# Regrouping the attention part of a fused attention and MLP kernel: two bursts a head in place of four

## The chip, the cores and the metric

The kernel runs on one core of a Trainium2 chip. The metric is the device time of one execution in microseconds (us). The engines are TensorE (PE in the profile, with its weight loads apart as PEld), VectorE (DVE), ScalarE (ACT), GpSimd (POOL) and SyncE (SP). Each runs its instructions in the order in which they were issued to it; a transfer is issued by one of their queues, nearly always SP's.

## The reference

```python
def _attn_ref(q, k, v, proj):              # 2 batches, 8 heads, 768 positions, 64 wide
    q_bits = (einsum('bhsd,dk->bhsk', q, proj) > 0)      # 6 bits; k_bits in the same way
    mask = q_bucket[:, :, :, None] == k_bucket[:, :, None, :]
    scores = where(mask, 1/sqrt(D) * q @ k.T, -1e9)
    attn = exp(scores - scores.max(-1))
    return attn / (attn.sum(-1) + 1e-9) @ v
# x: (1536, 512), the heads side by side
x = g1(x @ w_in) @ w_out        # 512 -> 2048 -> 512, g1(h) = h * tanh(softplus(h))
y = g2(x @ w2_in) @ w2_out      # the same sizes, g2 a rational function of h
```

## The kernel before

The attention part takes the first third of the time: 16 heads, one behind the other. The two MLP layers follow as 96 steps of 24 matmuls (3 blocks of 512 tokens, 16 slices of the hidden width, 2 layers).

**Numbers.** A large matmul splits each operand into a high and a low fp32r half and adds three products. The products P·V, the denominators and the hash codes are plain fp32, for which TensorE runs two instructions each. They use part of its columns: P·V (`both`, L285) and the codes two tiles of 64 columns side by side, the denominators (`dsum`, L400) four tiles of 32.

**Slots.** A head has six slots (`order`, L539, and the loop under it). Slot g of the whole run holds a list of operations, in the order of the rows of `order`; a row's first number says at which slot, counted from the head's own first, it stands, and its second how many there are (0: one for two heads). `slot_ops(g)` issues them, so each engine's queue has them in this order. In each slot TensorE computes a chunk of 128 keys of one head: `st` (L373) makes the scores `sp`, and ScalarE takes their exp `e`. For a later head, `smax` (L340) makes the products `mp`, whose row maxima VectorE reduces (`m`). Scores, maxima's products and a small sum of V (`vsum`, L268, tile `vsp`, read by VectorE as `vsc`) take turns in three PSUM buffers of two banks (`ps`, L181). P·V has one bank (`pv`), and the codes and denominators share one (`dn`, L182).

**Where things stand.** Per head, P·V stands in slots 3, 5 and 7, two chunks each; the denominators in slots 5 (two pairs of chunks) and 7 (one); the codes of a later head in slot 2 modulo 6 (`codes`, L298), with `code_k` on VectorE (L320) in the same slot and `code_q` on ScalarE (L329) two slots later. `hi` and `lo` split a head's q and k. `move_k`, `move_x` and `move_h` (L239 to L251) copy the halves between partitions by transfers. `fin_a` and `fin_b` (L354, L362) send the maxima back as a row of `qB`, through SP and GpSimd. `evac` and `devac` (L414, L427) take P·V and the denominators out of PSUM, and `gather`, `recip`, `store` and `spread` turn the latter into a factor for each position. For each pair of heads `norm`, `xhi` and `xlo` (L478 to L499) write the halves of the MLP's input; `norm` and `xhi` stand in slot 11 modulo 12, `xlo` in 5, `vsum` in 3. `weights` (L517) converts 14 parts of the MLP's weights, one a head: load, three VectorE instructions, split on GpSimd.

**Beginning and end.** `start` (L603) is a list by hand that prepares heads 0 to 2, with small products (`warm`) between. `tail` (L626) issues the last slots, from 99 on, within steps 1, 2 and 4 of the MLP; there VectorE also converts the rest of the first layer's weights (`direct_bits`, L777), which come through a ring of loads.

Of the kernel before, what the change touches and what calls it, by code (L numbers as in the profile page):

```python
# [9 lines left out]
F32 = mybir.dt.float32  # L10
# [16 lines left out]
BIG = 2.0 ** 40  # L27
NBITS = 6
EARLY, SHARED, FIRST = 7, 3, (78, 66, 72, 60, 60, 60, 60)
W_AT, W_LEAD = 7, 4  # L30
POOL_LO = (("lo", 1), ("lo", 2))
ENG = dict(
    lo="dd", hi="aa", xhi="a", xlo="dd", whi="pppp", wlo="pppp",
# [11 lines left out]
def attention_moe_moe(ctx: ExitStack, tc: tile.TileContext, kq, v, proj2, cst, eye, w1, w2, ab, out):  # L45
# [124 lines left out]
    def attention(actx, tctx):  # L170
# [26 lines left out]
        def memsets():  # L197
            nc.vector.memset(ones, 1.0)
            nc.vector.memset(wones, 1.0)
            nc.gpsimd.memset(cs_t, 0.0)  # L200
            nc.gpsimd.memset(cs_t[:, 1:2], -1.0)
            nc.gpsimd.memset(cs_t[:, 2:3], 1.0)
            for i in range(4):
                nc.gpsimd.memset(f32(KK[i])[32:64, 0], 0.0)
            for i in range(2):
                nc.gpsimd.memset(f32(SM[i]), 0.0)
            nc.gpsimd.memset(bias[:, 1:2], 1.000001)
# [25 lines left out]
                fn = fn or lo_of("lo", h)  # L233
                fn(qX[h % 4], raws[h], qB[h % 4])

        def khi(h, i):
            nc.scalar.activation(out=KK[h % 4][64:128, i], in_=raws[h][0:64], func=ACT.Copy)

        def move_k(h):  # L239
            if 0 <= h < B * H:  # L240
# [53 lines left out]

        ct = {}


        def codes(h):  # L298
            if not 0 <= h < B * H:
                return  # L300
            ct[h] = [pvp.tile([128, 512], F32, tag="dn", name="cp")] * 2
            if h == 0:
                ct[h][1] = pvp.tile([128, 512], F32, tag="pv", name="wm")
            for t in ct[h][0:1 + (h == 0)]:
                both(t, p_raw, raws[h], start=True, stop=True)


        warm_up = []

        def warm(n):  # L310
            if 0 in ct:
                t = ct[0][1]
            else:
                if not warm_up:
                    warm_up.append(ps.tile([128, 2, 512], F32, tag="s", name="wm"))
                t = warm_up[0][:, 0]
            for _ in range(n):
                nc.tensor.matmul(out=t[0:32, HALF:512], lhsT=ones, rhs=wones, start=True, stop=True)

        def code_k(h):  # L320
            if not 0 <= h < B * H:
                return
            for a in range(2):
                nc.vector.tensor_scalar(
                    out=qhalf(KK[h % 4][0:32, 0], a), in0=ct[h][0][64 * a:64 * a + 32, 0:HALF],
                    scalar1=cs_t[:, 1:2], scalar2=cs_t[:, 2:3], op0=ALU.is_gt, op1=ALU.mult,
                )

        def code_q(h):  # L329
            if not 0 <= h < B * H:  # L330
                return
            for a in range(2):
                nc.scalar.activation(
                    out=qhalf(qB[h % 4], a)[0:32], in_=ct[h][1][64 * a + 32:64 * a + 64, 0:HALF],
                    func=ACT.Sign, bias=cs_t[:, 0:1],
                )

        mt = {}

# [58 lines left out]


        def dsum(h, c):  # L400
            if not 0 <= h < B * H or c % 2 == 0:
                return
            if c == 1:
                pvt[h, "d"] = pvp.tile([128, 512], F32, tag="dn", name="dn")
            for n in range(4):
                nc.tensor.matmul(  # L406
                    out=pvt[h, "d"][32 * n:32 * n + 32, 0:HALF], lhsT=ones, rhs=qhalf(pt[h, c - 1 + n // 2], n % 2),
                    start=(c == 1), stop=(c == NC - 1),
                )

        Rt = {}
# [15 lines left out]
        def devac(h):  # L427
            if not 0 <= h < B * H:
                return
            dv = cs_p.tile([128, HALF], F32, tag="dv", name="dv")  # L430
            nc.scalar.activation(out=dv, in_=pvt.pop((h, "d"))[:, 0:HALF], func=ACT.Copy)
            Rt[h] = dv

        def gather(h):
            if not 0 <= h < B * H:
                return
            dv = Rt.pop(h)
            cs = cs_p.tile([24, 2, 32], F32, tag="cs", name="cs")
            for n in range(2):
                nc.sync.dma_start(  # L440
                    out=cs[:, n], in_=dv[64 * n:64 * n + 64:32].rearrange("t (a i) -> t a i", i=32)
                )
            Rt[h] = cs

        def recip(h):
            if not 0 <= h < B * H:
                return
            cs = Rt.pop(h)
            rc = cs_p.tile([24, 32], F32, tag="rc", name="rc")

            z = cs_p.tile([24, 32], F32, tag="z", name="z")
            nc.vector.tensor_tensor(out=rc, in0=cs[:, 0], in1=cs[:, 1], op=ALU.add)
            nc.vector.tensor_scalar(
                out=z, in0=rc, scalar1=0.0, scalar2=float(np.float32(1e-9)) / (S * TINY) - 1.0, op0=ALU.is_equal, op1=ALU.mult
            )
            nc.vector.tensor_scalar(out=rc, in0=rc, scalar1=1e-9, scalar2=None, op0=ALU.add)
            nc.vector.reciprocal(out=rc, in_=rc)
            nc.vector.scalar_tensor_tensor(out=rc, in0=z, scalar=1.0, in1=rc, op0=ALU.add, op1=ALU.mult)
            Rt[h, "r"] = rc
# [64 lines left out]
        def first(f, n):  # L524
# [16 lines left out]
            ("smax", smax, -11, 6),  # L541
            ("fin_a", fin_a, -5, 1),
            ("fin_b", fin_b, -5, 1),
            ("hi", hi, -18, 1),
            ("move_k", move_k, -17, 1),
            ("lo", lo, -15, 1),
            ("codes", codes, -16, 1),
            ("pv", pv, (3, 3, 5, 5, 7, 7), 6),
            ("dsum", dsum, (5, 5, 5, 5, 7, 7), 6),
            ("vsum", vsum, 3, 0),  # L550
            ("code_k", code_k, -16, 1),
            ("code_q", code_q, -14, 1),
            ("evac", evac, 7, 1),
            ("devac", devac, 7, 1),
            ("gather", gather, 8, 1),
            ("recip", recip, 10, 1),
            ("store", store, 11, 1),
            ("spread", spread, 12, 1),
            ("norm", norm, 23, 0),
            ("xhi", xhi, 23, 0),  # L560
            ("xlo", xlo, 29, 0),
            ("vred", vred, -6, 0),
            ("move_x", move_x, -13, 1),
            ("move_h", move_h, -11, 1),
# [2 lines left out]
            ("weights", weights, 0, -1),  # L567
            ("first", first, FIRST, -2),
        )
        last = 6 * nh + 3  # L570
        slots = {}
        done = set()
        for name, fn, at, per in order:
# [3 lines left out]
                todo = [(at[c] + 6 * h, (h, c)) for h in range(nh) for c in range(per)]  # L577
            elif name == "smax":
                todo = [((at, c - 2, 4 + c)[h] if h < 3 else at + 6 * h + c, (h, c)) for h in range(nh) for c in range(per)]
            elif name.startswith("fin_"):  # L580
                todo = [((at, 3, 9)[h] if h < 3 else at + 6 * h, (h,)) for h in range(nh)]
            elif per > 0:
                todo = [(at + 6 * h + c, (h, c) if per > 1 else (h,)) for h in range(nh) for c in range(per)]
            elif per == 0:
                todo = [(at + 12 * j, (j,)) for j in range(nh // 2)]
            else:
                todo = [(g, (g,)) for g in range(6 * nh)]
# [7 lines left out]

        def get(i):
            t, d = ((p_raw, proj2), (cs_t[0:31], cst[0:31]), (ab_t, ab))[i]
            nc.sync.dma_start(out=t, in_=d)

        def coef():  # L600
            nc.scalar.activation(out=babs, in_=ab_t[:, 4:6], func=ACT.Abs)

        start = (  # L603
            ("load", 0), ("get", 0), ("get", 1), ("load", 1), ("load", 2), ("warm", 5), ("hi", 0), ("codes", 0),
            ("khi", 0, 0), ("lo", 0), ("code_q", 0), ("code_k", 0), ("warm", 1), ("hi", 1), ("lo", 1), ("khi", 0, 1),
            ("get", 2), ("move_x", 0), ("smax", 0, 0), ("warm", 2), ("move_h", 0), ("hi", 2), ("lo", 2), ("smax", 0, 1),
            ("move_k", 1), ("warm", 2), ("smax", 0, 2), ("load", 3), ("warm", 2), ("smax", 0, 3), ("codes", 1),
            ("smax", 0, 4), ("warm", 2), ("code_q", 1), ("smax", 0, 5), ("fin_a", 0), ("fin_b", 0), ("code_k", 1),
            ("warm", 6), ("move_k", 2), ("load_v", 0), ("move_x", 1), ("smax", 1, 0), ("smax", 1, 1), ("move_h", 1),
            ("coef",),  # L610
        )

        def run():
            memsets()
            fns = {o[0]: o[1] for o in order}
            fns.update(get=get, coef=coef, khi=khi)
            for name, *k in start:
                if name == "warm":
                    warm(*k)
                    continue  # L620
                done.add(("move_k" if name == "khi" else name, tuple(k[:1]) if name == "khi" else tuple(k)))
                fns[name](*k, **({"fn": lo_pool} if (name, *k) in POOL_LO else {}))
            for g in range(last):
                slot_ops(g)

        def tail(i):  # L626
            for g in {1: range(last, last + 3), 2: range(last + 3, last + 5), 4: range(last + 5, last + 30)}.get(i, ()):
                slot_ops(g)

        return run, tail  # L630
# [1 line left out]
    def moe(mctx, tctx, tail):  # L632
# [114 lines left out]
        def run():  # L747
# [70 lines left out]
            for i in range(-5, len(seq) + 5):  # L818
# [20 lines left out]
                        fn(*k)  # L839
                if i >= 0:  # L840
                    tail(i)
                if i == 4:
                    tctx.close()
                for group in ((ring_store, slot_lo, direct_lo), (slot_both, slot_f32, direct_load, ring_load)):
                    for fn, k in now:
# [75 lines left out]
```

## Time and profile before

| | |
|---|---|
| median of 3 runs | 793.95 us (792.95 to 795.28) |
| the profiled execution | 791.69 us, span 789.8 |
| PE, PEld busy | 774.2 us (98%), 572.4 us (72%) |
| DVE, ACT, POOL busy | 593.7 us, 422.5 us, 71.6 us |
| chain that ended last | PE 88%, DVE 6%, DMA 2% |
| attention, MLP | to 259.65 us, from there to the end |

Times in the profile's views are us from the beginning of the span. A busy share alone doesn't say whether an engine runs well: TensorE may be busy with products that change its tiling, and a wait may lie on the one engine that sets the end. An instruction in a line is named by engine, source line, and "out<-in" of its tiles; "x8" says that eight in a row were merged.

### The profile page before, as it was taken

How to read it: one execution, taken by the hardware profiler on the slowest of the kernel's cores; microseconds unless marked ns; L12 is line 12 of the kernel's file. 1: busy time of each engine (PE TensorE's matmuls, PEld its weight loads, DVE VectorE, ACT ScalarE, POOL GpSimd, SP SyncE). 2: the span in 40 equal slices, each digit the busy share in tenths (PEclk: the TensorE clock that was granted, in tenths of full speed). 3: DMA queues.
4: the chain of work that ended last, by engine and by line, in shares of the span. 5: the costliest groups of instructions: out<-in, count | busy, mean ns of one | idle time of the engine just before them, and what ended most of it. 6: DMA issues, size and time to landing. Idle time of an engine off the chain costs nothing.

```text
span 789.8 us, 10934 instructions
## 1 busy us (share of the span) xinstructions
PE 774.2 (98%) x3788; PEld 572.4 (72%) x3788; DVE 593.7 (75%) x1100; ACT 422.5 (53%) x684; POOL 71.6 (9%) x100
## 2 busy tenths in 40 slices
PE   7899999999999999999999999999999999999998
PEld 4556555555555778888888888887888888888886
DVE  5587778778772599846556677659998888888886
ACT  3455565655555443331212334368886867777664
POOL 4223214124121000000000000000000000000000
PEclk9999999999999999999999999999999999999999
DMA  4847666554651444424555587620000100000001
GB/s 124 211 128 202 174 162 175 141 142 121 174 166 31 127 137 148 131 87 145 171 157 149 165 255 256 202 80 1 0 1 1 53 1 1 1 36 18 1 0 54
DMA packets 57031, 85.50 MB, mean 108 GB/s; under 512 B 20496, under 2 KB 28688, under 8 KB 56976
## 3 DMA queue, kind: packets, MB, share of 16 engines
q1 hardware_dynamic: 55952, 84.77, 36.4%
q8 instruction: 30, 0.49, 0.3%
q14 instruction: 25, 0.20, 0.1%
q0 software_dynamic: 1024, 0.03, 0.1%
HBM read 57.71 MB, written 14.73 MB: 92 GB/s over the span
## 4 chain that ended last, share of the span: by engine, by line
PE 88%; DVE 6%; DMA 2%; ACT 1%; issue 1%; SPq 1%; POOL 0%; DVEq 0%; ACTq 0%
PE h L665 29%; PE y L685 16%; PE y L683 15%; PE sp L380 9%; PE pv L287 8%; PE mp L347 5%; PE dn L406 4%; PE cp L287 2%; DVE w L70 1%; DVE m L351 1%; DMA kk<-qB 1%; DVE t L103 1%; DMA vf<-v 1%; DVE r L106 1%; DVE gl L70 1%
## 5 line engine op out<-in xcount | busy, mean ns | idle before, releaser
L665 PE MATMUL h<-xh,w 128*128 128x512 f32 x768 | 205.0, 389 | 0.0
L665 PEld LDWEIGHTS h<-xh,w 128*128 128x128 f32 x768 | 144.1, 188 | 30.6 <-issue 0.6
L351 DVE TENSOR_REDUCE m<-mp 128x1 f32<-128x768 f32 x96 | 91.3, 955 | 50.2 <-PE mp L347 49.0
L385 ACT ACTIVATE e<-sp 128x768 f32<-128x768 f32 x96 | 77.1, 810 | 80.8 <-PE sp L380 79.4
L70 DVE TENSOR_TENSOR gl<-ep,gh 128x512 fp32r<-128x512 f32 x96 | 65.9, 687 | 69.4 <-ACT ep L709 68.6
L708 ACT ACTIVATE gh<-h 128x512 fp32r<-128x512 f32 x48 | 28.7, 598 | 154.7 <-PE h L665 141.5
L665 PE MATMUL h<-xl,w 128*128 128x512 f32 x384 | 102.7, 389 | 0.0
L685 PE MATMUL y<-w,gh 128*128 128x512 f32 x384 | 96.3, 389 | 0.0
L683 PE MATMUL y<-gh,w 128*128 128x512 f32 x384 | 94.8, 389 | 0.0
L665 PEld LDWEIGHTS h<-xl,w 128*128 128x128 f32 x384 | 72.1, 188 | 15.1
L683 PEld LDWEIGHTS y<-gh,w 128*128 128x128 f32 x384 | 72.1, 188 | 15.0
L685 PEld LDWEIGHTS y<-w,gh 128*128 128x128 f32 x384 | 72.1, 188 | 15.0
L287 PE MATMUL pv<-e,vf 128*64 128x384 f32 x384 | 72.5, 499 | 0.0
L380 PE MATMUL sp<-qB,kk 128*128 128x384 f32 x192 | 55.5, 370 | 1.6 <-DMA qB<-stt 1.1
L715 ACT ACTIVATE ep<-h 128x512 f32<-128x512 f32 x48 | 28.5, 595 | 52.3 <-PE h L665 52.3
L347 PE MATMUL mp<-kk,qB 128*128 128x384 f32 x192 | 52.8, 358 | 3.2 <-DVE m L351 2.3
L106 DVE SCALAR_TENSOR_TENSOR r<-r,t 128x256 int32<-128x256 int32 (+1 forms) x114 | 52.2, 457 | 4.7
L380 PEld LDWEIGHTS sp<-qB,kk 128*128 128x128 f32 x192 | 30.8, 188 | 34.1 <-issue 16.0
L103 DVE SCALAR_TENSOR_TENSOR t<-r,t 128x256 int32<-128x256 int32 (+1 forms) x114 | 52.2, 458 | 3.9
L685 PE MATMUL y<-w,gl 128*128 128x512 f32 x192 | 53.3, 392 | 0.5 <-DVE gl L70 0.4
L717 DVE TENSOR_TENSOR n<-n,ep 128x512 f32<-128x512 f32 x48 | 33.1, 690 | 26.9 <-ACT n L716 26.9
L683 PE MATMUL y<-gl,w 128*128 128x512 f32 x192 | 51.6, 390 | 1.6 <-DVE gl L70 1.6
(79 smaller groups left out, 1012.2 us busy)
## 6 DMA issues: line engine op xcount, KB each, us to landing
r<-w SPq DMA_DIRECT2D x100, 256.0 KB
w<-r SPq DMA_DIRECT2D x64, 128.0 KB
w<-w SPq DMA_DIRECT2D x16, 512.0 KB
r<-w SPq DMA_DIRECT2D x14, 512.0 KB
kq<-kq SPq DMA_DIRECT2D x16, 384.0 KB
kk<-qB SPq DMA_DIRECT2D x15, 384.0 KB
kk<-qX SPq DMA_DIRECT2D x16, 192.0 KB
qX<-qB SPq DMA_DIRECT2D x16, 192.0 KB
```

The costliest lines, as they stand in the source:

```text
L70: nc.vector.tensor_tensor(out=o, in0=i, in1=f32(h), op=ALU.subtract)
L103: lambda: nc.vector.scalar_tensor_tensor(out=t, in0=r[:, :, 1], scalar=-0x40000000, in1=t, op0=ALU.bitwise_and, op1=ALU.bitwise_or),
L106: lambda: nc.vector.scalar_tensor_tensor(out=o, in0=r[:, :, 0], scalar=29, in1=t, op0=ALU.logical_shift_right, op1=ALU.bitwise_or),
L287: nc.tensor.matmul(out=o[64 * a:64 * a + 64, 0:HALF], lhsT=w, rhs=qhalf(x, a), start=start, stop=stop)
L347: nc.tensor.matmul(out=p[:, a, 0:HALF], lhsT=qB[h % 4][:, c * 128:(c + 1) * 128], rhs=qhalf(KK[h % 4][:, 0], a), start=True, stop=True,)
L351: nc.vector.tensor_reduce(out=mt[h][:, c:c + 1], in_=halves(p), op=ALU.max, axis=AX.XY)
L380: nc.tensor.matmul(out=p[:, a, 0:HALF], lhsT=kk[:, c * 128:(c + 1) * 128], rhs=qq[:, a * HALF:(a + 1) * HALF], start=(i == 0), stop=(i == 1),)
L385: nc.scalar.activation(out=wide(e), in_=halves(p), func=ACT.Exp, scale=1.0 / D ** 0.5)
L665: nc.tensor.matmul(out=p, lhsT=w[:, c * 128:(c + 1) * 128], rhs=x[:, c, :], start=(n == 0), stop=(n == 11))
L683: nc.tensor.matmul(out=y[m], lhsT=w[:, DM + m * 128:DM + (m + 1) * 128], rhs=g, **s)
L685: nc.tensor.matmul(out=y[m], lhsT=g[:, m * 128:(m + 1) * 128], rhs=w[:, DM:2 * DM], **s)
L717: nc.vector.tensor_tensor(out=v_, in0=v_, in1=u, op=ALU.mult)
```

## The change

The order of slots, the beginning and the end are rewritten; what is computed stays.

- P·V and denominators of a head stand in two slots, 5 and 8, with three chunks each. The codes of a later head stand in front of P·V in slot 5 and write the two banks of one of the three score buffers. `signs` makes them into k's and q's codes in the same slot, VectorE on one bank while ScalarE is on the other.
- The denominators of one chunk are four products of 192 columns, not those of two chunks four of 384. So `gather` is one transfer, and `recip` has one addition less.
- `evac`, `devac`, `gather` stand one slot later, `recip`, `store`, `spread` four, `norm`, `xhi`, `xlo` three, `vsum` one earlier; `lo` stands behind `vsum` and `recip` in the order within a slot. The loads of heads 4 and 5 stand in slots 1 and 3; the weights' conversion two slots earlier.
- The list `start` is new: head 0 is split by three engines, the projection is loaded through ScalarE's queue, there are fewer warm-up products. The tail's slots, from 100 on, are issued in steps 2, 3 and 5.

```diff
-W_AT, W_LEAD = 7, 4
+W_AT, W_LEAD = 5, 4
...
+            nc.gpsimd.memset(f32(qB[0])[32:64], 0.0)
...
-        def khi(h, i):
-            nc.scalar.activation(out=KK[h % 4][64:128, i], in_=raws[h][0:64], func=ACT.Copy)
+        def khi(i):
+            o = KK[0][64:128, i] if i < 2 else qX[0][0:64]
+            nc.scalar.activation(out=o, in_=raws[0][0:64], func=ACT.Copy)
+
+        def qhi():
+            nc.vector.tensor_copy(qB[0][64:128], raws[0][64:128])
+
+        def qlo():
+            lo_pool(qX[0][64:128], raws[0][64:128], qB[0][64:128])
+
+        def klo():
+            lo_pool(qX[0][0:64], raws[0][0:64], qX[0][0:64])
...
+        def code_products(h):
+            for a in range(2):
+                nc.tensor.matmul(
+                    out=ct[h][a][64 * a:64 * a + 64, 0:HALF], lhsT=p_raw, rhs=qhalf(raws[h], a), start=True, stop=True
+                )
...
-            ct[h] = [pvp.tile([128, 512], F32, tag="dn", name="cp")] * 2
-            if h == 0:
-                ct[h][1] = pvp.tile([128, 512], F32, tag="pv", name="wm")
-            for t in ct[h][0:1 + (h == 0)]:
-                both(t, p_raw, raws[h], start=True, stop=True)
+            p = ps.tile([128, 2, 512], F32, tag="s", name="cp")
+            ct[h] = p[:, 0], p[:, 1]
+            code_products(h)
...
+        def signs(h):
+            for a in range(2):
+                code_k(h, (a,))
+                code_q(h, (1 - a,))
...
         def dsum(h, c):
-            if not 0 <= h < B * H or c % 2 == 0:
-                return
-            if c == 1:
+            if not 0 <= h < B * H:
+                return
+            if c == 0:
                 pvt[h, "d"] = pvp.tile([128, 512], F32, tag="dn", name="dn")
             for n in range(4):
                 nc.tensor.matmul(
-                    out=pvt[h, "d"][32 * n:32 * n + 32, 0:HALF], lhsT=ones, rhs=qhalf(pt[h, c - 1 + n // 2], n % 2),
-                    start=(c == 1), stop=(c == NC - 1),
+                    out=pvt[h, "d"][32 * n:32 * n + 32, 0:S // 4], lhsT=ones,
+                    rhs=pt[h, c][:, n * S // 4:(n + 1) * S // 4], start=(c == 0), stop=(c == NC - 1),
                 )
...
-            for n in range(2):
-                nc.sync.dma_start(
-                    out=cs[:, n], in_=dv[64 * n:64 * n + 64:32].rearrange("t (a i) -> t a i", i=32)
-                )
+            nc.sync.dma_start(out=cs, in_=dv[0:128:32].rearrange("t (a i) -> t a i", i=32))
...
-            nc.vector.tensor_tensor(out=rc, in0=cs[:, 0], in1=cs[:, 1], op=ALU.add)
...
-            ("hi", hi, -18, 1),
-            ("move_k", move_k, -17, 1),
-            ("lo", lo, -15, 1),
-            ("codes", codes, -16, 1),
-            ("pv", pv, (3, 3, 5, 5, 7, 7), 6),
-            ("dsum", dsum, (5, 5, 5, 5, 7, 7), 6),
-            ("vsum", vsum, 3, 0),
-            ("code_k", code_k, -16, 1),
-            ("code_q", code_q, -14, 1),
-            ("evac", evac, 7, 1),
-            ("devac", devac, 7, 1),
-            ("gather", gather, 8, 1),
-            ("recip", recip, 10, 1),
-            ("store", store, 11, 1),
-            ("spread", spread, 12, 1),
-            ("norm", norm, 23, 0),
-            ("xhi", xhi, 23, 0),
-            ("xlo", xlo, 29, 0),
+            ("hi", hi, -19, 1),
+            ("move_k", move_k, -18, 1),
+            ("codes", codes, -13, 1),
+            ("pv", pv, (5, 5, 5, 8, 8, 8), 6),
+            ("dsum", dsum, (5, 5, 5, 8, 8, 8), 6),
+            ("vsum", vsum, 2, 0),
+            ("signs", signs, -13, 1),
+            ("recip", recip, 14, 1),
+            ("lo", lo, -16, 1),
+            ("evac", evac, 8, 1),
+            ("devac", devac, 8, 1),
+            ("gather", gather, 9, 1),
+            ("store", store, 15, 1),
+            ("spread", spread, 16, 1),
+            ("norm", norm, 26, 0),
+            ("xhi", xhi, 26, 0),
+            ("xlo", xlo, 32, 0),
...
-        last = 6 * nh + 3
+        last = 6 * nh + 4
...
+            elif name == "load":
+                todo = [(at + 6 * h if h > 5 else 2 * h - 7, (h,)) for h in range(nh)]
...
-            nc.sync.dma_start(out=t, in_=d)
+            (nc.sync if i else nc.scalar).dma_start(out=t, in_=d)
...
+            ("get", 0), ("load", 0), ("get", 1), ("load", 1), ("load", 2), ("warm", 5), ("khi", 0), ("qhi",), ("codes", 0),
+            ("warm", 4), ("signs", 0), ("khi", 2), ("qlo",), ("hi", 1), ("klo",), ("khi", 1), ("get", 2), ("smax", 0, 0),
+            ("warm", 1), ("move_k", 1), ("move_x", 0), ("lo", 1), ("smax", 0, 1), ("warm", 1), ("hi", 2), ("lo", 2),
+            ("smax", 0, 2), ("warm", 1), ("move_h", 0), ("load", 3), ("smax", 0, 3), ("warm", 1), ("smax", 0, 4),
+            ("warm", 1), ("move_x", 1), ("smax", 0, 5), ("codes", 1), ("fin_a", 0), ("fin_b", 0), ("signs", 1),
+            ("move_h", 1), ("load_v", 0), ("move_k", 2), ("warm", 5), ("smax", 1, 0), ("smax", 1, 1), ("coef",),
...
-            for g in {1: range(last, last + 3), 2: range(last + 3, last + 5), 4: range(last + 5, last + 30)}.get(i, ()):
+            for g in {2: range(last, last + 5), 3: range(last + 5, last + 7), 5: range(last + 7, last + 30)}.get(i, ()):
...
-                if i == 4:
+                if i == 5:
                     tctx.close()
```

## Rows read from the trace of the kernel before

**Rows 1.** The page, part 1: busy us (share of the span), instructions of each engine.

```profile
PE 774.2 (98%) x3788; PEld 572.4 (72%) x3788; DVE 593.7 (75%) x1100; ACT 422.5 (53%) x684; POOL 71.6 (9%) x100
```

**Rows 2.** Windows of heads 7 and 8: length, each engine's busy us, clock, DMA.

```profile
128.64:143.40 14.76, 14.76 (x92) 8.24 (x89) 12.80 (x22) 8.47 (x13) 3.95 (x5) 1.00 0.50 142
143.40:159.12 15.72, 15.37 (x97) 8.73 (x93) 11.89 (x22) 9.03 (x14) 4.93 (x7) 1.00 0.55 149
```

**Rows 3.** Chain that ended last, heads 7 and 8: start, us, what.

```profile
128.71 0.91 PE sp L380 x4
129.63 0.35 PE mp L347 x2
129.98 0.70 PE sp L380 x4
130.68 0.46 PE mp L347 x2
131.14 1.44 PE pv L287 x8
132.58 0.78 PE dn L406 x8
...
134.62 0.80 PE cp L287 x4
...
142.04 1.43 PE dn L406 x16
...
153.39 0.54 PE vsp L274 x4
```

**Rows 4.** Timeline of DVE, heads 7 and 8: start, us, instruction.

```profile
140.48 0.17 DVE L453 TENSOR_SCALAR z<-rc 24x32 f32<-24x32 f32 x1
...
141.38 0.94 DVE L351 TENSOR_REDUCE m<-mp 128x1 f32<-128x768 f32 x1
142.24 0.94 DVE L482 TENSOR_TENSOR xf<-ev,R 128x768 f32<-128x768 f32 x1
...
153.05 0.95 DVE L70 TENSOR_TENSOR qX<-kq,qB 128x768 fp32r<-128x768 f32 x1
153.97 0.16 DVE L279 TENSOR_SCALAR vsc<-vsp 128x2 f32<-128x2 f32 x1
```

**Rows 5.** Timeline of ACT, end of head 7 and beginning of head 8.

```profile
143.21 0.94 ACT L61 ACTIVATE xh<-xf 128x512 fp32r<-128x512 f32 x2 [1.26 <-DVE xf L482]
144.40 0.81 ACT L385 ACTIVATE e<-sp 128x768 f32<-128x768 f32 x1 [0.25 <-PE sp L380]
```

**Rows 6.** Timeline of PE, head 8; in brackets idle before it and its releaser.

```profile
145.78 0.61 PE L347 MATMUL mp<-kk,qB 128*128 128x384 f32 x2 [0.35 <-DVE m L351]
```

**Rows 7.** Timeline of PE, the beginning: small products on one tile of 32 columns.

```profile
14.93 1.50 PE L318 MATMUL wm<-wones,ones 128*32 128x128 f32 x12
```

**Rows 8.** A window of 0.03 us, PE's instructions on tile `dn` alone.

```profile
127.21:127.24 0.03, 0.02 (x4) 1.00 2.45 341
```

**Rows 9.** Chain that ended last, the beginning and the first MLP step.

```profile
1.19 2.84 DMA pr<-proj
...
18.96 4.72 DMA vf<-v
...
28.23 5.62 DMA kk<-qB
...
262.25 4.03 DMA r<-w
```

**Rows 10.** Timeline of PE and ACT, the beginning and the MLP's fifth step.

```profile
19.67 0.59 PE L380 MATMUL sp<-qB,kk 128*128 128x384 f32 x2 [1.05 <-DMA qB<-stt]
...
33.93 1.16 ACT L333 ACTIVATE qB<-cp,cst 32x384 fp32r<-32x384 f32 x2 [3.37 <-DMA kk<-qB]
...
35.15 1.50 PE L406 MATMUL dn<-e,ones 128*32 128x384 f32 x16 [1.76 <-ACT qB L333]
...
290.79 1.21 PE L683 MATMUL y<-gl,w 128*128 128x512 f32 x4 [1.60 <-DVE gl L70]
```

More of the change, by code (lines that the diff above doesn't have):

```diff
@@ L300, in codes, with code_k, code_q @@
                 return
-            ct[h] = [pvp.tile([128, 512], F32, tag="dn", name="cp")] * 2
-            if h == 0:
-                ct[h][1] = pvp.tile([128, 512], F32, tag="pv", name="wm")
-            for t in ct[h][0:1 + (h == 0)]:
-                both(t, p_raw, raws[h], start=True, stop=True)
+            p = ps.tile([128, 2, 512], F32, tag="s", name="cp")
+            ct[h] = p[:, 0], p[:, 1]
+            code_products(h)
         warm_up = []
         def warm(n):
[L311 to L316, printed above, removed]
+            if not warm_up:
+                warm_up.append(pvp.tile([128, 512], F32, tag="pv", name="wm"))
             for _ in range(n):
-                nc.tensor.matmul(out=t[0:32, HALF:512], lhsT=ones, rhs=wones, start=True, stop=True)
-        def code_k(h):
+                nc.tensor.matmul(out=warm_up[0][0:32, 0:128], lhsT=ones, rhs=wones, start=True, stop=True)
+        def code_k(h, of=(0, 1)):
             if not 0 <= h < B * H:
                 return
-            for a in range(2):
+            for a in of:
                 nc.vector.tensor_scalar(
-                    out=qhalf(KK[h % 4][0:32, 0], a), in0=ct[h][0][64 * a:64 * a + 32, 0:HALF],
+                    out=qhalf(KK[h % 4][0:32, 0], a), in0=ct[h][a][64 * a:64 * a + 32, 0:HALF],
                     scalar1=cs_t[:, 1:2], scalar2=cs_t[:, 2:3], op0=ALU.is_gt, op1=ALU.mult,
                 )
-        def code_q(h):
+        def code_q(h, of=(0, 1)):
             if not 0 <= h < B * H:
                 return
-            for a in range(2):
+            for a in of:
                 nc.scalar.activation(
-                    out=qhalf(qB[h % 4], a)[0:32], in_=ct[h][1][64 * a + 32:64 * a + 64, 0:HALF],
+                    out=qhalf(qB[h % 4], a)[0:32], in_=ct[h][a][64 * a + 32:64 * a + 64, 0:HALF],
                     func=ACT.Sign, bias=cs_t[:, 0:1],
                 )
+        def signs(h):
+            for a in range(2):
+                code_k(h, (a,))
+                code_q(h, (1 - a,))
         mt = {}
@@ L429, in devac @@
                 return
-            dv = cs_p.tile([128, HALF], F32, tag="dv", name="dv")
-            nc.scalar.activation(out=dv, in_=pvt.pop((h, "d"))[:, 0:HALF], func=ACT.Copy)
+            dv = cs_p.tile([128, S // 4], F32, tag="dv", name="dv")
+            nc.scalar.activation(out=dv, in_=pvt.pop((h, "d"))[:, 0:S // 4], func=ACT.Copy)
             Rt[h] = dv
@@ L437, in gather @@
             dv = Rt.pop(h)
-            cs = cs_p.tile([24, 2, 32], F32, tag="cs", name="cs")
-            for n in range(2):
-                nc.sync.dma_start(
-                    out=cs[:, n], in_=dv[64 * n:64 * n + 64:32].rearrange("t (a i) -> t a i", i=32)
-                )
+            cs = cs_p.tile([24, 32], F32, tag="cs", name="cs")
+            nc.sync.dma_start(out=cs, in_=dv[0:128:32].rearrange("t (a i) -> t a i", i=32))
             Rt[h] = cs
@@ L451, in recip @@
             z = cs_p.tile([24, 32], F32, tag="z", name="z")
-            nc.vector.tensor_tensor(out=rc, in0=cs[:, 0], in1=cs[:, 1], op=ALU.add)
             nc.vector.tensor_scalar(
-                out=z, in0=rc, scalar1=0.0, scalar2=float(np.float32(1e-9)) / (S * TINY) - 1.0, op0=ALU.is_equal, op1=ALU.mult
+                out=z, in0=cs, scalar1=0.0, scalar2=float(np.float32(1e-9)) / (S * TINY) - 1.0, op0=ALU.is_equal, op1=ALU.mult
             )
-            nc.vector.tensor_scalar(out=rc, in0=rc, scalar1=1e-9, scalar2=None, op0=ALU.add)
+            nc.vector.tensor_scalar(out=rc, in0=cs, scalar1=1e-9, scalar2=None, op0=ALU.add)
             nc.vector.reciprocal(out=rc, in_=rc)
@@ L603, in attention @@
         start = (
[L604 to L610, printed above, removed]
+            ("get", 0), ("load", 0), ("get", 1), ("load", 1), ("load", 2), ("warm", 5), ("khi", 0), ("qhi",), ("codes", 0),
[4 more added lines that the diff above has]
+            ("move_h", 1), ("load_v", 0), ("move_k", 2), ("warm", 5), ("smax", 1, 0), ("smax", 1, 1), ("coef",),
         )
@@ L615, in run @@
             fns = {o[0]: o[1] for o in order}
-            fns.update(get=get, coef=coef, khi=khi)
+            fns.update(get=get, coef=coef, khi=khi, qhi=qhi, qlo=qlo, klo=klo, signs=signs)
+            done.update((name, (0,)) for name in ("hi", "lo", "move_k", "code_k", "code_q"))
             for name, *k in start:
@@ L620, in run @@
                     continue
-                done.add(("move_k" if name == "khi" else name, tuple(k[:1]) if name == "khi" else tuple(k)))
+                done.add((name, tuple(k)))
                 fns[name](*k, **({"fn": lo_pool} if (name, *k) in POOL_LO else {}))
```

## The prediction

> **What bounds the kernel now.** I read the page's busy shares first: TensorE (PE) is busy 98% of the span [rows 1], so what counts is the length of its instruction stream and the places where it waits. Then I cut the attention part at the first score product of each head and asked for the stretches: an odd head takes 14.76 us with TensorE never idle, an even one 15.72 with 15.37 busy [rows 2]. Nothing off TensorE is worth anything there unless it makes TensorE wait. Then the chain of waits through two heads gives the prices [rows 3]. In a slot the scores `sp` take 0.70 and the maxima's products `mp` 0.35. Directly behind a burst of other products `sp` takes 0.91, so going back costs 0.20. Four code instructions take 0.80 and eight P·V instructions 1.44: 0.16 each and 0.16 to begin. Eight and sixteen denominator instructions take 0.78 and 1.43: 0.081 each and 0.13 to begin. So a burst costs 0.36 beyond its work, and there are four a head: P·V with denominators in slots 1 and 5, codes in slot 2, P·V in slot 3.
>
> **The change, part by part.**
>
> *Two bursts.* Slots 2 and 5 now hold everything: 12 P·V and 24 (half as wide) denominator instructions, in slot 5 with the 4 code ones ahead. Where three slots run together, TensorE needs 0.91+0.35+0.70+0.35+0.70+0.35 = 3.36. It has three score buffers, so its fourth product waits for the first exp and the fifth for the first maximum. Counted from the first `sp`: the exp starts at 1.0 (144.40 for the head that begins at 143.40 [rows 2, 5]), takes 0.81 and ends 1.85; TensorE is there at 1.96, so it just touches that wait and may pay a restart. The second `mp` of a pair shows this price now: 0.46 and, in other pairs, 0.51 to 0.54 against 0.35 [rows 3]. The maximum starts at some 1.4, when its products have drained, takes 0.94 [rows 4] and ends 2.35, where TensorE arrives. Two such touches a run at 0.11 to 0.19: I take 0.27 (bounds 0 and 0.4). P·V: 0.16+12×0.16 = 2.08, with codes 2.72, as both use 64-column tiles.
>
> *Denominators by quarters.* 24 instructions of 192 columns in place of 12 of 384. No row shows 192. If time follows columns, each is 0.0405 and a burst's share 0.13+24×0.0405 = 1.10, as for 12 old ones. The low end is this; the high end is no shrinking at all, 24×0.081+0.13 = 2.07 (+0.97 in each of 32 bursts, +31). The nearest row is 12 products of 128 columns on one tile in 1.50 [rows 7], 0.125 each with the drain, so 192 columns are at most 0.19 for four tiles side by side: 1.27, +5.4 in all. I take 1.10, because four such products begin within 0.03 us [rows 8], so issue does not hold them. The Trainium skill (TensorE: Matmul & The Clock Gate, "Wait — 56ns, not 53.3ns?") says that without hardware decode the sequencer spends about 62 ns on every matmul; by that a burst's share would be 24×0.062 = 1.49, +0.39, and the sum +12.5 us. The four in 0.03 us speak against it here; the measurement decides.
>
> An odd head is then 2×3.36+2.08+2.72+2×1.10+2×0.27 = 14.26, against 14.76: -0.5. Five of them (3 to 11): -2.5.
>
> *Even heads.* These add `vsp` (0.54), which also the old ones have: 14.80 without anything new. But the order within a slot is changed. In slots 26, 38, 50, 62 and 74 (2 modulo 12) there now meet `vsum`, `recip`, `lo`, `norm` and `xhi`, and on VectorE they stand in that order. `vsc`, the first, waits for `vsp`, which TensorE reaches only behind the whole burst. Before, `lo` stood ahead of it (rows 153.05 and 153.97) and `norm` with `xhi` six slots away [rows 4]. Walked from the first `sp` of the head: the run ends at 3.6, P·V at 5.7, denominators at 6.8, `vsp` at 7.35, its result is read at 7.5. VectorE has been done with its maximum since 4.8 and stood still. Then come `recip` 0.90 (140.48 to 141.38), `lo` 0.92 (153.05 to 153.97), `norm` 0.94 [rows 4]: 10.3. ScalarE holds `xhi` (0.94 [rows 5]) until then, and the next slot's exp is queued behind `xhi`: exp from 11.3 to 12.1. The next slot's maximum is queued behind `norm`: 10.3 to 11.3. TensorE meanwhile has filled its three buffers by 9.2 and stands. It gets one at 11.3 and the other at 12.2, and ends the run at 13.5 to 13.9, where 10.9 was due. So 2.6 to 3.0 of stall; I take 2.8. Bounds: 0, if exp and maximum weren't held, and 3.5, if `vsp` comes late by its own 0.54. A stall of this kind, a product waiting for a maximum, is in the trace at 0.35 [rows 6]. Even head: 17.6 against 15.72, +1.9; five of them +9.4. Head 2 has `vsum`, `recip` and `lo` without `norm`: the maximum comes at 9.4 instead of 8.7, so +0.8-0.5 = +0.3. In head 14 there are no maxima, so three exps fit the three buffers and nothing waits. Heads 1, 13, 14 and 15, counted in the same way (codes or maxima missing, half of a head's P·V carried over into the next instead of a third), come out even within 0.5.
>
> Steady part: -2.5+9.4+0.3 = **+7.2**.
>
> *Codes in the scores' banks.* They leave the denominators' bank; the signs are made by both engines at once, within the burst behind them (2.72+1.10 us against 1.3 of signs): nothing, as that buffer is wanted only by the fifth product of the next run. Its cover is the burst; without it a buffer would be missing for 1.3.
>
> *Beginning.* The first scores start at 19.67 [rows 10]. Four code products instead of eight before the first maximum, one warm-up product between maxima instead of two (so that the reduction sets the pace), and ScalarE, VectorE and GpSimd sharing head 0's splits give some 1.5; the projection's load, 2.84 to land [rows 9], goes behind ScalarE's table load and takes up to 0.8 back. First scores at about 18.0. But SP now issues V's load ahead of head 2's `move_k`, and V's took 4.72 to land [rows 9]; the signs of head 2 on ScalarE wait for `move_k`, about 22.9, and hold the second exp till 24, about where it is now, and in addition the code tile now keeps a score buffer till then. What stays is the stall of 1.76 at 35.15, where the denominators wait for signs that ScalarE could make only when `move_k` of head 3 had landed (5.62 behind two loads) [rows 9, 10]: the bank is no longer shared, and the loads of heads 4 and 5 move to slots 1 and 3, behind `move_k`. Late next is the maxima's row of head 1 (`fin_b`), queued on SP behind head 4's load, a ring load now two slots earlier, and V's second load. I come to head 1 at 33.8 instead of 36.6 (35.15 and the 1.43 of sixteen denominator instructions [rows 3, 10]): **-2.8** (bounds -6, if no transfer holds it, and +1).
>
> *End.* One gather and one shorter eviction less in front of the ring's loads; VectorE waits for the first of these, 4.03 us [rows 9], now some 1.0 sooner. It then runs without a gap until TensorE waits 1.60 at 290.79 [rows 10]; `norm` and `xlo` of the last pair move to step 5, which has two ring pieces instead of three. **-1.6** (bounds -1.8 and +0.5).
>
> **Sum.** -2.8+7.2-1.6 = +2.8. The profiled execution took 791.69 us (span 789.8), so 794.5 in its terms; the median of the runs is 793.95, 2.3 higher, so I forecast 796.7.
>
> **Rivals.** (A) Faster: the held exps and maxima cost little, because VectorE reads `vsp` earlier than I think or the delayed run catches up. Without the 5×2.8 and 0.8 the sum is -12, 782; with half of it -5, 789. For: odd heads are never idle now, so each burst saved counts. Against: both queues are in order, and 14.76 with 92 products has no slack to catch up in. The point is 1.8 us of stall a time: below that it is faster by more than 2.4. (B) Narrow products don't shrink as columns do: at 0.19 for 192 columns it is +5.4 and 802, and unshrunk +31 and 828. For: no row has such a product. Against: [rows 8]. A fall of TensorE's clock in stalls of three microseconds would count on the same side; the granted clock is 1.00 in both stretches of [rows 2], with 0.35 of idle in all, so no row here prices it. (C) The beginning decides: it keeps its whole 6 and stalls are 2.6: -1.4, 792.5, no change; or head 1 waits for `fin_b` still longer and nothing is won, 800.
>
> **Chances.** Forecast 0.50, A 0.28, B 0.10, C 0.12. A time within 0.3% (2.4 us) can't be told from no change. The forecast's own range is 792 to 802: slower 0.30, same 0.17, faster 0.03. A gives faster 0.26, same 0.02; B slower 0.10; C slower 0.03, same 0.06, faster 0.03. Together faster 0.32, same 0.25, slower 0.43. With A's lower half and B's upper part left out, the range is 784 to 804.
>
> **What would show it.** Odd heads at 14.2 to 14.4 from first `sp` to first `sp`: bursts priced rightly; 15 or more: the quarters are dear. Even heads 4 to 12 near 17.6, with TensorE idle some 2 us in the fourth slot, released by ScalarE's exp or VectorE's maximum, and VectorE idle before `vsc`: the stall. Even heads at 14.8 make the forecast wrong, and A right. Head 1's first score product near 33.8, and no wait at `y` near 290: beginning and end.

## The result and the profile after

The changed kernel takes 799.44 us (median of 4 runs, 798.96 to 799.99), the one before 794.62 (4 runs, 792.95 to 796.20): ratio 1.0068 [1.0041, 1.0096]. It is slower by 4.8 us. The profiled execution took 799.11 us with a span of 797.3, 7.5 more than before in span; before's profiled execution lay 2.9 below its median, this one 0.3.

Part 1 of the page after: busy us (share), instructions of each engine, as [rows 1].

```profile
PE 772.6 (97%) x4166; PEld 590.3 (74%) x4166; DVE 584.4 (73%) x1084; ACT 421.5 (53%) x684; POOL 73.6 (9%) x103
```

TensorE is 1.6 us less busy than before and the span is 7.5 longer, so it idles for 9.1 us more; its busy time also holds products that ran at the lower clock (below). I cut both executions at the same places:

| | before | after | difference | forecast |
|---|---|---|---|---|
| first score product | 19.67 | 20.06 | +0.4 | -1.7 |
| from there to head 1 | 16.90 | 19.90 | +3.0 | -1.1 |
| heads 1 to 15 | 223.07 | 229.03 | +6.0 | +7.2 |
| first MLP product to the end | 530.1 | 528.3 | -1.8 | -1.6 |

The forecast was 796.7 (784 to 804) and slower: the time lies in the range, 2.7 above it. In the terms of one execution it was +2.8, and +7.5 came: the beginning was missed by 6.2, and the heads, mostly the even ones, were priced 1.2 too high.

Windows of head 7 and head 8 of the kernel after, columns as in [rows 2]:

```profile
135.70:149.98 14.28, 14.28 (x116) 9.18 (x113) 10.59 (x20) 8.34 (x12) 3.00 (x4) 1.00 0.38 105
149.98:166.90 16.92, 14.98 (x120) 9.55 (x116) 11.37 (x21) 8.94 (x14) 5.22 (x7) 1.00 0.56 151
```

The odd head is 0.48 shorter than in [rows 2] and TensorE is never idle in it. The even head is 1.20 longer and TensorE stands for 1.94. Its chain (start, us, what) names what stood in between:

```profile
139.40 2.09 PE pv L299 x12
141.49 1.11 PE dn L424 x24
...
146.21 0.80 PE cp L311 x4
147.00 1.94 PE pv L299 x12
...
155.75 1.11 PE dn L424 x24
156.87 0.55 PE vsp L286 x4
...
157.44 0.16 DVE vsc L291
...
157.79 0.35 DVE rc L471
...
158.35 0.87 DVE qX L70
159.22 0.88 DVE xf L496
...
160.65 0.40 ACT xh L61
161.05 0.71 ACT e L403
...
161.80 0.98 PE sp L398 x4
```

The upper lines are the bursts: 12 P·V and 24 denominator instructions take 3.20, with four code instructions 3.85. The lower ones are the queue that was forecast: `vsc` waits for the whole burst, `recip`, `lo` and `norm` stand behind it on VectorE, `xhi` and then the exp behind them on ScalarE. The same stretch, as timelines of DVE and of PE (in brackets idle and its releaser):

```profile
157.44 0.16 DVE L291 TENSOR_SCALAR vsc<-vsp 128x2 f32<-128x2 f32 x1 [2.76 <-PE vsp L286]
...
160.01 0.94 DVE L369 TENSOR_REDUCE m<-mp 128x1 f32<-128x768 f32 x1
```

```profile
161.01 0.62 PE L365 MATMUL mp<-kk,qB 128*128 128x384 f32 x2 [1.76 <-DVE m L369]
161.80 0.62 PE L398 MATMUL sp<-qB,kk 128*128 128x384 f32 x2 [0.17 <-ACT e L403]
```

VectorE is idle for 2.76 us and then runs `vsc`, `recip`, `lo`, `norm` and the maximum in a row. TensorE stands for 1.76 until that maximum gives a buffer back. [rows 6] showed the same wait at 0.35.

The beginning after: its chain, then five rows of the timeline (SPq and POOL are issues of transfers by SP and GpSimd), and one row of the timeline of before.

```profile
14.89 0.21 DVE stt L378
...
16.39 3.47 DMA qB<-stt
...
20.06 0.99 PE sp L398 x4
21.05 5.32 DMA kk<-qB
...
27.79 0.58 ACT qB L345
...
28.42 1.65 PE sp L398 x4
```

```profile
14.65 0.46 SPq L263 DMA_DIRECT2D qX<-qB  x1
...
15.72 1.20 POOL L384 DMA_DIRECT2D qB<-stt  x2 [1.09 <-DVE kk L336]
...
16.40 1.57 SPq L384 DMA_DIRECT2D qB<-stt  x2
...
26.48 0.58 ACT L345 ACTIVATE qB<-cp,cst 32x384 fp32r<-32x384 f32 x1 [3.85 <-DMA kk<-qB]
...
28.42 1.01 PE L398 MATMUL sp<-qB,kk 128*128 128x384 f32 x2 [3.50 <-ACT qB L345]
```

```profile
17.13 1.25 POOL L366 DMA_DIRECT2D qB<-stt  x2 [4.47 <-DVE kk L324]
```

Two transfers set it. The first is the row of maxima of head 0, which `fin_b` sends in four pieces of 0.8 KB, two through GpSimd and two through SP. It was ready (end of `stt`) at 15.10, 1.4 us sooner than before (16.53), but the first score came 4.96 us after that, not 3.14. SP stood at `move_h` of head 0 until 14.65, then issued a load and a move, and came to its two pieces 1.3 us late, at 16.40 and 17.27. GpSimd issued its two 0.6 and 1.3 us after `stt`, as in the kernel before, but behind that load and move they took 3.5 us each to land, against 1.6 and 1.7 before; the last of them, issued at 16.39, is the one in the chain. Then head 2's `move_k`, issued behind V's load, landed at 26.37. The signs waited for it, the code tile they read is now one of the three score buffers, and the third slot's scores waited 3.50 for that buffer. At the end no wait at `y` is left, where [rows 10] had 1.60.

Windows of the beginning after; the third number from the end of a line is TensorE's granted clock.

```profile
14.00:20.00 6.00, 2.52 (x18) 1.66 (x14) 3.83 (x7) 1.24 (x3) 1.82 (x3) 1.00 0.46 134
20.00:25.00 5.00, 4.85 (x16) 2.94 (x16) 1.79 (x3) 1.54 (x2) 0.26 (x1) 0.66 0.83 202
25.00:30.00 5.00, 1.58 (x5) 1.58 (x6) 1.63 (x2) 1.96 (x3) 1.90 (x3) 0.76 0.59 124
30.00:35.00 5.00, 5.00 (x20) 5.00 (x19) 3.23 (x6) 1.91 (x3) 0.00 (x0) 0.56 0.98 290
```

TensorE was busy for 2.52 of the 6 us ahead of 20.0 and for 1.58 of the 5 between 25.0 and 30.0. The records show its clock at the lower level (1.2 of 2.4 GHz) from 20.79 to 24.20 and from 27.62 to 34.44: the four products of a score take 1.65 us there, against 0.91 in [rows 3]. Before, the same four stretches show 1.00.

### The profile page after: what moved, and what is told of

It reads as the page before. It is cut to its first block, busy times and chain, and to the rows that moved or that the text cites. A ratio compares the mean times of both kernels' runs of the same rounds, so it can differ in the third digit from the quotient of the medians.

```text
span 797.3 us, 11677 instructions
## 1 busy us (share of the span) xinstructions
PE 772.6 (97%) x4166; PEld 590.3 (74%) x4166; DVE 584.4 (73%) x1084; ACT 421.5 (53%) x684; POOL 73.6 (9%) x103
## 4 chain that ended last, share of the span: by engine, by line
PE 86%; DVE 7%; DMA 3%; ACT 2%; issue 1%; SPq 0%; POOL 0%; DVEq 0%; ACTq 0%
PE h L680 29%; PE y L700 16%; PE y L698 14%; PE sp L398 9%; PE pv L299 8%; PE dn L424 4%; PE mp L365 4%; PE cp L311 2%; DMA r<-w 1%; DVE m L369 1%; DVE w L70 1%; ACT e L403 1%; DMA kk<-qB 1%; DVE xf L496 1%; DVE qX L70 1%
## 5 line engine op out<-in xcount | busy, mean ns | idle before, releaser
L299 PE MATMUL pv<-e,vf 128*64 128x384 f32 x384 | 69.2, 496 | 0.0
L299 PEld LDWEIGHTS pv<-e,vf 128*64 128x64 f32 x384 | 26.2, 138 | 33.4 <-issue 33.2
```

The costliest lines, as they stand in the source:

```text
L299: nc.tensor.matmul(out=o[64 * a:64 * a + 64, 0:HALF], lhsT=w, rhs=qhalf(x, a), start=start, stop=stop)
```

## The experiments

**Control.** The changed kernel once more.

> The changed kernel as it is, on the same chip as the others of this call. Both theories: 1.0068 of the kernel before within 0.3%, odd heads at 14.26 us and even heads at 16.9 from first score product to first score product, some of them at 18.5 where the granted clock falls behind the stall.

Measured: 798.83 us, ratio 1.0065 [1.0044, 1.0086]; heads 1 to 15 229.0, as in the table. But its clock rose only at about 20: six maxima's products follow each other at 1.50 us instead of 0.88, the first score comes at 22.18, and head 1 at 39.15. Of the eleven profiled executions with the new beginning four show the first rise before 8 us (at 5.2 to 7.8; one of these fell back at once) and seven at 18 to 21; where `move_k` is not moved as below, head 1 comes late in both sorts (38.2 to 40.0, against 36.57 before). In the control the row was ready only at 18.67. GpSimd issued its pieces at 19.26 and 19.94, with that load landed (19.1) and the move nearly (19.8), and they landed in 1.7 and 1.6 us, as before. Both profiled executions with the old beginning (before's, and the last experiment's) show it by 7.0; the second has a fall from 19.4 to 22.8 and reaches head 1 at 36.33 nevertheless.

**The row `vsum` behind `xhi`.** One line of `order` moved:

```diff
-            ("vsum", vsum, 2, 0),
             ...
             ("xhi", xhi, 26, 0),
+            ("vsum", vsum, 2, 0),
```

> The changed kernel with one row moved: vsum stands behind xhi in the order within a slot, so VectorE does recip, lo and norm before it waits for vsp. Theory (queue order): even heads 4 to 12 fall from 16.92 to 14.8 to 15.1 us from first score product to first score product, since exp and maximum of the next slot are no longer held behind xhi and norm; with head 2 some 10 us less in all, about 789. Rival (three slots in a row are too much for three score buffers, whatever the order): even heads stay at 16.9 and the time at 799.

Measured: 791.38 us, .9992 [.9976, 1.0008]; heads 1 to 15 221.8 instead of 229.0. So the position of `vsc` in VectorE's queue costs 7.2 us of the profiled spans (1.6 of it is the control's one fall of the clock, in head 6), and some 6 by the ratios of the runs: the forecast's mechanism is the cause. But even heads are 14.70, 16.95, 15.73, 15.73, 14.70 and not all near 14.8. Chain of the one of 16.95:

```profile
115.19 0.71 PE sp L398 x4
...
115.98 0.82 ACT e L403
...
116.85 0.97 PE sp L398 x4
```

Here a score product waits for the exp of the very score product in front of it. With three buffers in turn it would wait for an earlier one. So it seems that the program, which fixes the buffer of each tile, gave the same one twice running; the strict turn below tests it. That is a second cause, which the forecast didn't have.

**The row `lo` ahead of `vsum`.**

```diff
+            ("lo", lo, -16, 1),
             ("vsum", vsum, 2, 0),
             ...
-            ("lo", lo, -16, 1),
```

> The changed kernel with lo alone moved ahead of vsum, as it stood before; recip, norm and xhi stay behind it. Theory (the wait for vsp heads a chain recip, lo, norm, xhi, and each link counts): the chain is shorter by lo's 0.92, even heads 4 to 12 at 16.0 and head 2 0.5 shorter, some 5 us less in all, about 794. Rival (norm and xhi alone hold the next slot, or the buffers do): even heads at 16.9 as in the changed kernel, 799.

Measured: 793.07 us, 1.0010 [.9991, 1.0030]. Even heads 16.03, 16.66, 16.66, 16.04, 16.04: with one 0.92 us operation fewer behind `vsc`, the shortest ones are 0.9 below 16.92, and the wait for the maximum's buffer is 0.89 instead of 1.76. The stall goes with the length of the queue behind `vsc`; the two of 16.66 have in addition a score that waits 0.43 for the exp right before it, as above.

**Head 2's `move_k` earlier.** In the list `start`:

```diff
-    ... ("smax", 0, 2), ("warm", 1), ("move_h", 0), ...
-    ("move_h", 1), ("load_v", 0), ("move_k", 2), ("warm", 5), ...
+    ... ("smax", 0, 2), ("warm", 1), ("move_k", 2), ("move_h", 0), ...
+    ("move_h", 1), ("load_v", 0), ("warm", 5), ...
```

> The changed kernel with one entry of the beginning's list moved: move_k of head 2 is issued before move_h of head 0, when SP waits anyway, and not behind V's load. Theory (the beginning is late because head 2's signs wait for this transfer, which landed at 26.4): the wait of 3.5 us on TensorE in slot 2 goes, TensorE's clock does not fall there, head 1's first score product comes at 35 to 36.5 instead of 39.96, 3.5 to 5 us less in all, about 795. Rival (another wait takes its place, for V's sum or for the row of maxima of head 1): head 1 at 38.5 or later, 798.

Measured: 797.37 us, 1.0052 [1.0033, 1.0070]; head 1 at 37.47 instead of 39.2 to 40.0. ScalarE's first sign of head 2 starts at 25.16, behind VectorE's, and waits for no transfer. So `move_k` held the beginning, though for less than its wait: 35 to 36.5 and a full clock were forecast, and the clock still fell, from 17.6 to 24.4. In the time alone the gain is not clear of the control's interval. Late next is the maxima's row of head 1, from its chain:

```profile
32.35 0.32 SPq L384
...
32.71 4.63 DMA qB<-stt
...
37.47 0.95 PE sp L398 x4
```

**Small products against the clock's fall.** Five in front of the first score and fourteen in front of slot 2:

```diff
-    ... ("smax", 1, 1), ("coef",),
+    ... ("smax", 1, 1), ("warm", 5), ("coef",),
...
+                if g == 2:
+                    warm(14)
```

> The changed kernel with 5 warm-up products more behind the last maxima's products of the beginning and 14 in front of slot 2, so that TensorE has something to do while it waits. Theory (the half clock from 20.8 to 24.2 and from 27.6 to 34.4 costs time): the granted clock stays at 1.00 to 130 us and head 1's first score product comes 3 to 4 us sooner, at 36 to 37; 795.5. Rival (the slots there are set by ScalarE, VectorE and transfers, so the clock costs nothing): head 1 at 39.5 to 40.3 with a full clock, 799.

Measured: 799.71 us, 1.0081 [1.0054, 1.0107]: nothing won. In the profiled execution the clock stayed full from 18.5 to 97.1 and head 0 took 15.93, against 16.97 in the control. But the first score came at 23.48 instead of 22.18, and head 1 at 39.42. The small products take in front what the clock gives behind, so the clock of slots 2 to 4 alone is not where the beginning is lost.

**Both repairs**: `vsum` behind `xhi` and `move_k` early.

> The changed kernel with vsum behind xhi in the order within a slot, and head 2's move_k issued ahead of head 0's move_h. Theory (two separate losses, in the queue order of slot 2 and in the beginning): the two gains of the single runs add, 1.0068 less 0.75% less 0.2%: 0.997 of the kernel before, head 1 at 37 to 38. Rival (both lose to the same fall of TensorE's clock, so that one of the two moves already brings the whole): no better than vsum alone, 0.999.

Measured: 788.96 us, .9939 [.9919, .9959]; heads 1 to 15 223.5, head 1 at 36.45. It is faster than the kernel before, and than the 0.997 to which the two single gains add up. The even heads are 14.72, 18.66, 15.74, 15.73, 14.70; in the one of 18.66 the granted clock is 0.91, behind waits of the kind shown above.

**Codes back in the denominators' bank.**

```diff
-            p = ps.tile([128, 2, 512], F32, tag="s", name="cp")
-            ct[h] = p[:, 0], p[:, 1]
+            p = pvp.tile([128, 512], F32, tag="dn", name="cp")
+            ct[h] = p, p
```

> The changed kernel with the codes' products in the denominators' bank, as before the change, both halves in the one bank; everything else as changed. Theory (the codes' own banks are what lets them stand in front of a burst): the denominators of slot 5 wait for the signs, which take 2.6 us on two engines in turn where P.V covers 1.9, so that some 0.7 to 0.9 us are added in each of 13 heads: odd heads at 15.0 to 15.2, about 10 us more in all, ratio 1.018 to 1.022. Rival (P.V hides the signs in any bank, and the code tile only takes a score buffer away): odd heads at 14.2, ratio 1.005 to 1.007.

Measured: 811.58 us, 1.0216 [1.0181, 1.0251], odd heads 15.20 to 15.22, even ones 17.84 to 19.34. Its chain in an odd head shows the cover that the prediction named, gone:

```profile
84.75 0.44 DVE kk L336
...
85.41 0.59 ACT qB L345
...
86.02 0.68 DVE kk L336
...
86.73 0.58 ACT qB L345
...
87.36 1.16 PE dn L424 x21
```

VectorE and ScalarE take turns: their four signs take 2.6 us and not 1.3. The codes' place in the scores' banks is therefore a condition of the two bursts, worth about 13 us here, two more falls of the clock than in the control among them.

**`norm` and `xhi` in slot 29**, with `recip` and `lo` ahead of `vsum`, and `move_k` early.

> The changed kernel with recip and lo ahead of vsum, norm and xhi in slot 29 instead of 26 (5 modulo 12, with the signs and the weights' conversion), and head 2's move_k issued early. Theory (any slot whose burst covers VectorE's work is good for norm): even heads at 14.8 to 15.2, since nothing of the next slot stands behind vsc any more; ratio 0.993 to 0.997. Rival (VectorE is full in slot 5 too, and the stall only moves there, behind signs, norm and conversion): even heads at 15.7 or more, ratio 1.000 or more.

Measured: 794.18 us, 1.0020 [.9998, 1.0042]. Even heads 14.70, 16.57, 16.55, 15.32, 14.69, odd ones up to 16.11. It takes the queue behind `vsc` away in another way, and the heads still scatter by up to 1.9 us. From head 4 on each wait of TensorE over 0.2 us is a score (0.43) or a maximum's product (0.96) that waits for an exp. So the scatter is not that queue, nor a VectorE that is full in slot 5 (the rival), though the time is the rival's. This pointed to the buffers. One of the ten executions took 967.89 us, which nothing here explains.

**Three buffers strictly in turn**, on top of the two repairs:

```diff
+        turn = []
+
+        def score_buf(name):
+            turn.append(name)
+            return ps.tile([128, 2, 512], F32, tag=f"s{len(turn) % 3}", name=name, bufs=1)
...
-            p = ps.tile([128, 2, 512], F32, tag="s", name="sp")
+            p = score_buf(name="sp")
```

and likewise for `mp`, `vsp` and `cp`.

> The kernel with both moves (vsum behind xhi, head 2's move_k early), and the three score buffers given out strictly in turn, by three tags of one buffer each. Theory (what is left of the long even heads comes from the order in which the planner gave out the buffers: in heads 6, 8 and 10 a score product waits for the exp of the one just before it): all even heads from 4 to 12 at 14.7 to 14.8 instead of 14.7, 18.7, 15.7, 15.7, 14.7, no fall of the clock after head 1, some 5 us less, ratio 0.986 to 0.989. Rival (exp or the maximum is late there whatever the buffer): heads 6 to 10 as before, ratio 0.994.

Measured: 784.19 us (783.53 to 785.85), .9879 [.9851, .9907], the fastest version. Heads 1 to 15 take 216.96. Windows of its heads 7 and 8:

```profile
128.01:142.43 14.42, 14.42 (x117) 9.17 (x113) 11.99 (x21) 8.34 (x12) 3.11 (x5) 1.00 0.68 164
142.43:157.12 14.69, 14.69 (x120) 9.58 (x116) 11.45 (x21) 9.18 (x14) 5.37 (x7) 1.00 0.52 132
```

No idle time is left in either; even heads 4 to 12 are all 14.69 to 14.71.

**The strict turn alone in each kernel.** The same function in the changed kernel as it was, and in the kernel before (for `sp`, `mp`, `vsp` and its `wm`).

> The changed kernel with the three score buffers strictly in turn. Theory (the stall of an even head was walked with buffers in turn at 2.6 to 3.0 and measured at 2.1 because the planner gave the fourth product the buffer that came free first): even heads at 17.4 to 17.8 instead of 16.9, odd heads 14.26, 2 to 4 us more, ratio 1.009 to 1.012. Rival (the stall ends with the exp in any case): even heads at 16.9, ratio 1.0065.

> The kernel before with the three score buffers strictly in turn. Theory: the 0.35 of idle in its even heads, a product that waits for the maximum of the one just before it, goes, even heads at 15.2 to 15.3 instead of 15.72, some 3 us less, ratio 0.996. Rival: no change in the heads, ratio 1.000.

Measured: after with it 801.94 us, 1.0101 [1.0074, 1.0128], even heads 17.32 to 17.34 and, with the lower clock, 18.9; before with it 791.38, .9972 [.9950, .9993], even heads 15.21 to 15.22 and odd 14.75. In the kernel before the turn takes away the idle 0.35 of [rows 6], which was thus the order of the buffers. But the turn isn't a gain everywhere: while `vsc` blocks VectorE, the product next in turn waits for the exp and starts at 161.70, where it took the maximum's buffer at 161.01 before (heads that begin at 149.88 and 149.98), and the stall grows by 0.4. In the changed kernel it gives 4.8 us only with the queue repaired (788.96 to 784.19). And with the turn in both kernels, and the two repairs in the changed one, the regrouping is worth 784.19 against 791.38: 0.9% less; a pair of heads takes 29.11 against 29.96.

## Why the prediction was right, point by point

**Two bursts and quarters: right.** Forecast 14.26 an odd head, measured 14.25 to 14.28; P·V 2.08 against 2.09, codes and P·V 2.72 against 2.74, 24 denominator instructions 1.10 against 1.11. So columns set their price, and rival B is out. 1.11/24 is 46 ns each. The Trainium skill (TensorE: Matmul & The Clock Gate, "Wait — 56ns, not 53.3ns?") gives about 62 ns for each matmul with hardware decode off, an estimate of 1.49 for the burst; this trace, at 1.11, doesn't show that cost, and no run here shows which way its products are decoded.

**Even heads: the mechanism right, its size too large.** The wait stands in the slot forecast, at the product forecast, released by the maximum, with VectorE idle ahead of `vsc`; moving one row takes 7 us of the span away. Rival A, by which the held exps and maxima cost little, is out. The stall was put at 2.8 and measures 2.1 (16.92 less the 14.80 forecast for a head without it; such heads measure 14.70). The walk had TensorE get its buffers 11.3 and 12.2 us after the first score; they came at 11.0 and 11.8. That is the failed size of this term: 0.7 a head, less the 1.6 of one fall of the clock, which the prediction named without a price. The walk took the buffers in turn; with a strict turn an even head takes 17.32, so 0.4 of the 0.7 is the order in which the program gave them out.

**Codes in the scores' banks: right in sum, wrong in working.** "Both engines at once" and its 1.3 us are 2.6 us in turns. The burst of 3.05 covers it in a steady head; in the beginning, where a transfer is in front of the signs, nothing did.

**Beginning: the step that failed.** Forecast -2.8, measured +3.4 (+2.6 in the control). The engines' part of "first scores at about 18.0" came true: the row was ready at 15.10, and with the 3.14 us that its way took before that is 18.2. What failed is that the way was taken to stay the same. Because SP's queue stood at `move_h`, which waits for `move_x` to land, a load and a move went out right ahead of the row, and the way took 4.96. That these two slowed the pieces is argued from their order and from the control; no run changes it alone. `move_k` was seen to come late, at 22.9; it landed at 26.4. The stall of 1.76 ahead of head 0's denominators is gone, as forecast. And the prediction counted the code and small products that fall away only as time saved, while the runs show the clock low in two other stretches instead: behind the waits, or until about 20.

What `move_k` is worth depends on the clock. Where the clock rose early and did not fall back at once, head 1 came at 39.96 without the repair and at 37.47 and 36.45 with it; in the other executions of the new beginning at 38.2 to 39.6 in the six without and at 38.15 and 38.32 in the two with it, and these differ in other lines too. So 2.5 to 3.5 in the first sort, and from nothing to 1.4 in the second. The version with both repairs thus reached head 1 as early as the kernel before (36.57), but with the clock's rise early; the fastest one reaches it 1.6 us later. How the rest divides between the transfers and the clock isn't settled, nor which edit of the beginning keeps the clock low.

**End: right**, -1.8 against -1.6, with the wait at `y` gone.

Rival C was partly right too: in its losing branch nothing is won in the beginning, 800. The beginning did worse, and was held by head 2's `move_k` before the row of head 1 that C named. The smaller stalls gave back 1.2 of the 6.2 by which the beginning was missed, so the sum of parts was 4.6 too low (799.11 against 794.5). That the median lies only 2.7 above the forecast comes from the 2.3 added for the distance between profiled execution and median, which was 0.3 in the changed kernel. That is luck, and the range held because it was 20 us wide.

## What to carry to other kernels

Grouping products of one tiling pays what the chain's rows say, but the burst delays whatever waits on a product issued behind it: put such a reader last in its engine's order within the slot, since what stands behind it inherits the wait (here 0.9 us for each 0.9 us operation). When a stall goes and the periods still scatter, look at which product waits for which reader: buffers that don't come in strict turn can make a product wait for the one just ahead of it. A new beginning has to be walked through the issuing queue of the transfers too, instruction by instruction, as strictly as through the engines, and with what is still being carried when a small transfer goes out.

## What the runs showed of the hardware

The granted clock also fell in steady state, behind short waits. In head 6 of the changed kernel TensorE stood for 1.76 us and less, and from 130.02 to 133.43 the records show half speed; the head took 18.53 instead of 16.92, so one fall cost 1.6 us. The same wait in heads 4, 8, 10 and 12 had no fall behind it, and other executions had theirs at other heads. In the version with both repairs one came at 117.04 with no wait longer than 0.96 us just ahead of it.

VectorE and ScalarE, sent to the two banks of one tile, took turns: four signs of 0.6 to 0.7 us took 2.6 us (131.95 to 134.58 in the changed kernel), and the later waits of each were released by the other. Which rule of the program or the chip makes them wait isn't shown.

Head 0's pieces of 0.8 KB through GpSimd landed in 1.6 to 1.7 us in ten of the thirteen profiled executions. In the other three (the changed kernel, `move_k` early, both repairs) they took 3.5 to 4.0: the clock had risen early there, and the row came right behind a load and a move.
